# Gated linear attention and a max-out layer on one core: layer 2 per 128-token tile instead of per group of four

## The chip, the cores and the metric

The kernel runs on one core of one Trainium2 chip. The metric is the device time of one execution in microseconds (us); lower is better. Five engines take part: PE (matrix products), DVE (vector), ACT (activations), POOL (elementwise work beside DVE) and SP, which here issues every DMA. Each engine works through its own instructions strictly in program order and waits on semaphores for the others.

## The reference

q, k, v and f_logit are [4 batches, 8 heads, 768 tokens, 48]. A gated linear attention runs over the tokens, then a layer with two weight matrices, a maximum and an output product runs on its result x of [3072 tokens, 384].

```python
f = 1.0 / (1.0 + np.exp(-f_logit))
for t in range(S):
    state = f[:, :, t, :, None] * state + np.einsum('bhd,bhe->bhde', k[:, :, t], v[:, :, t])
    y[:, :, t] = np.einsum('bhd,bhde->bhe', q[:, :, t], state)
...
h1 = x @ w1
h2 = x @ w2
g = np.maximum(h1, h2)
return (g @ w_out).astype(np.float32)
```

w1 and w2 are [384, 1024], w_out is [1024, 384].

## The kernel before, in words

The work is cut into 24 tiles of 128 tokens. Tile i is chunk c = i // 4 of batch b = i % 4, so that four tiles in a row are the same chunk of the four batches, and the state of a batch is needed again four tiles later.

**Attention of a tile**, in six stages. `s_ell(i)` (L198 to L201): ACT makes e = exp(-f) and ell = ln(e + 1), the negative logarithm of the gate, and DVE casts v to vb. `s_cum(i)` (L208 to L221): PE sums ell over the tokens with a triangular matrix (cum, and four short matmuls for the total), ACT takes ei, ed and fl from it, and POOL scales k and q to kp and qp. `s_tr(i)` (L230, L234): PE transposes kp and qp in eight 128x128 pieces, and DVE copies them out as trs. `s_a(i)` (L245, L248): eight matmuls a, which DVE multiplies with the mask into am. `s_y(i)` (L260 to L280): the new state (sa on PE, tmp on DVE, st on POOL), then y from the old state and am, which ACT casts to x. `s_xT(i)` (L290, L291): three transposes of x, copied out by DVE as xT.

**Layer 2** uses max(h1, h2) = relu(h1 - h2) + h2. With wd = w1 - w2 and the product w2o = w2 @ w_out, the output is relu(x @ wd) @ w_out + x @ w2o. So the weights first go through preparation: w2 and w_out are cast, w2 is transposed (w2T, 24 transposes and 8 copies), w2o is multiplied (24 matmuls), wd is subtracted. After that a group of four tiles (512 tokens) takes 24 matmuls d of 512 columns (L156), eight relu casts gT on ACT (L158), and per tile 11 matmuls o of 384 columns (L172), a copy ob and an output DMA.

**Order.** The program order is the order in which the code calls the stages; nothing reorders it. A loop from i = -4 to 23 calls s_y(i), s_tr(i+2), s_a(i+1), s_cum(i+3), s_xT(i), s_ell(i+4) and load(i+8), and between them `unit()` takes the next piece of layer 2 from a queue: first the preparation pieces, then, after each fourth tile, the eight d and eight half o pieces of that group. The preparation pieces come before the first s_ell. What is left in the queue runs after the loop.

**Buffers.** The loaded q, k, v and f tiles have five buffers. In PSUM, a ring of three buffers (`ps_s`) serves cum, tr, sa, y and xtp, one (`ps_a`) serves a, and three (`ps_m`) serve layer 2. The input DMAs of tiles 0 to 2, then w2, w_out, tile 3, w1 and tile 4 are issued first.

Of the kernel before, what the change touches and what calls it, by code (L numbers as in the profile page):

```python
# [4 lines left out]

# [12 lines left out]
def kernel(  # L18
# [62 lines left out]
    ut = consts.tile([C, C], BF16)  # L81
    make_upper_triangular(nc, ut, 1.0, diag=True)
    ident = consts.tile([C, C], BF16)
    make_identity(nc, ident)
    ones_col = consts.tile([C, 1], BF16)
    nc.gpsimd.memset(ones_col, 1.0)
    NQ = 3
# [15 lines left out]
    w2_h = consts.tile([C, JG, d_ff], BF16, name="w2_h")
# [30 lines left out]
    for j in range(JG):
        units.append(lambda j=j: u_w2_cast(j))
    for h in range(4):
        units.append(lambda h=h: u_wo_cast(h))
    for f in range(FG):
        units.append(lambda f=f: u_w2T(f))
    for j in range(JG):  # L140
        units.append(lambda j=j: u_w2o(j))
    for j in range(JG):
        units.append(lambda j=j: u_wd(j))
    N_PREP = len(units)


    xT_g = {}

    def push_group(g):
        gT = work.tile([C, FG, GT], BF16, name="gT", tag="gT")  # L150
        xT = xT_g[g]

        def u_d(f):
            ps = ps_m.tile([C, GT], F32, name="d", tag="mm")
# [5 lines left out]
        hold = {}  # L160

        def u_o(b, half):
            ts = slice(b * C, (b + 1) * C)
            if half == 0:
                hold[b] = ps_m.tile([C, dm], F32, name="o", tag="mm")
            ps = hold[b]
            mms = [(xT[:, j, ts], w2o[:, j, :]) for j in range(JG)]
            mms += [(gT[:, f, ts], wo[:, f, :]) for f in range(FG)]
            cut = 6
            todo = range(0, cut) if half == 0 else range(cut, len(mms))  # L170
            for n in todo:
                nc.tensor.matmul(out=ps, lhsT=mms[n][0], rhs=mms[n][1],  # L172
                                 start=(n == 0), stop=(n == len(mms) - 1))
            if half == 1:
                ob = work.tile([C, dm], F32, name="ob", tag="ob", bufs=3)
                nc.vector.tensor_copy(ob, ps)  # L176
                r0 = b * S + g * C
                nc.sync.dma_start(out=out[r0:r0 + C, :], in_=ob)

        for f in range(FG):  # L180
            units.append(lambda f=f: u_d(f))
        for b in range(B):
            units.append(lambda b=b: u_o(b, 0))
            units.append(lambda b=b: u_o(b, 1))

    def unit(n=1):
        for _ in range(n):
            if units:
                units.popleft()()


    st = {}

    def s_ell(i):
        t = ld[i]
        e = work.tile([C, dm], F32, name="e", tag="e")
# [4 lines left out]
        nc.vector.tensor_copy(vb, t["v"].rearrange("p h d -> p (h d)"))  # L201
        st[i] = {"ell": ell, "v": vb}

    def s_cum(i):
# [76 lines left out]
        s["x"] = x  # L281

    def s_xT(i):
        c, b = divmod(i, B)
        s = st.pop(i)
        if b == 0:
            xT_g[c] = work.tile([C, JG, GT], BF16, name="xT", tag="xT", bufs=3)
# [3 lines left out]
        nc.vector.tensor_copy(xT_g[c][:, :, b * C:(b + 1) * C], ps)  # L291


    for i in range(-4, T):
        if i >= 0:
            s_y(i)
        unit()
        if 0 <= i + 2 < T:
            s_tr(i + 2)
        unit()  # L300
        if 0 <= i + 1 < T:
            s_a(i + 1)
        unit()
        if 0 <= i + 3 < T:
            s_cum(i + 3)
        unit()
        if i >= 0:
            s_xT(i)
        if i < B:
            unit()  # L310
            unit()
        if i >= 0 and i % B == B - 1:
            push_group(i // B)
        if 0 <= i + 4 < T:
# [35 lines left out]
```

## Time and profile before

| | us |
|---|---|
| median of 3 runs | 185.81 |
| lowest and highest of them | 185.0 and 186.49 |
| the profiled execution | 185.38 |
| its span, first to last instruction | 183.6 |
| PE busy in it | 138.6 |
| DVE, ACT, POOL busy | 102.5, 86.1, 75.7 |

An execution's time is a little longer than the span of its instructions. Busy times overlap between engines, so they don't add up to the span. Matmuls are pipelined: the row of one matmul shows its whole passage, and the spacing of starts shows the rate.

### The profile page before, as it was taken

How to read it: one execution, taken by the hardware profiler on the slowest of the kernel's cores; microseconds unless marked ns; L12 is line 12 of the kernel's file. 1: busy time of each engine (PE TensorE's matmuls, PEld its weight loads, DVE VectorE, ACT ScalarE, POOL GpSimd, SP SyncE). 2: the span in 40 equal slices, each digit the busy share in tenths (PEclk: the TensorE clock that was granted, in tenths of full speed). 3: DMA queues.
4: the chain of work that ended last, by engine and by line, in shares of the span. 5: the costliest groups of instructions: out<-in, count | busy, mean ns of one | idle time of the engine just before them, and what ended most of it. 6: DMA issues, size and time to landing. Idle time of an engine off the chain costs nothing.

```text
span 183.6 us, 3633 instructions
## 1 busy us (share of the span) xinstructions
PE 138.6 (75%) x1373; PEld 85.4 (46%) x1384; DVE 102.5 (56%) x161; ACT 86.1 (47%) x200; POOL 75.7 (41%) x107
## 2 busy tenths in 40 slices
PE   0000208946778989999999998999899988998992
PEld 0000106534555545655456654665556654564560
DVE  8200605389777576686676676766776744452031
ACT  2000074483555675446744577346873376412700
POOL 8200004646666366544466544566544644000000
PEclk9999999985555999999999999999999999999999
DMA  6999999999999997698996999969801120022022
GB/s 114 194 185 347 373 199 362 186 187 171 194 189 190 164 191 131 165 209 174 195 151 164 215 172 186 172 142 216 152 0 43 50 86 0 4 87 86 0 89 86
DMA packets 105154, 28.56 MB, mean 156 GB/s; under 512 B 100272, under 2 KB 104368, under 8 KB 105136
## 3 DMA queue, kind: packets, MB, share of 16 engines
q1 hardware_dynamic: 105136, 28.32, 77.1%
q8 instruction: 11, 0.18, 0.5%
q14 instruction: 7, 0.06, 0.1%
HBM read 23.59 MB, written 4.72 MB: 154 GB/s over the span
## 4 chain that ended last, share of the span: by engine, by line
issue 39%; PE 32%; POOL 23%; ACT 3%; POOLq 1%; DVE 1%; ACTq 0%
PE o L172 13%; POOL qp L221 11%; POOL kp L220 9%; PE d L156 9%; PE tr L230 6%; PE a L245 2%; POOL st L98 1%; ACT ei L216 1%; PE y L272 1%; ACT ed L217 1%; PE y L277 1%; ACT gT L158 1%; POOLq L345 1%; POOL ell L94 0%; PE cum L208 0%
## 5 line engine op out<-in xcount | busy, mean ns | idle before, releaser
L220 POOL TENSOR_TENSOR kp<-kt,ei 128x384 bf16<-128x384 f32 x24 | 24.9, 1036 | 76.4 <-issue 38.9
L156 PE MATMUL d<-xT,wd 128*128 128x512 bf16 x133 | 36.7, 383 | 2.3 <-DVE xT L291 1.1
L158 ACT ACTIVATE gT<-d 128x512 bf16<-128x512 f32 x48 | 29.0, 605 | 19.0 <-PE d L156 18.5
L172 PE MATMUL o<-wo,gT 128*128 128x384 bf16 x192 | 37.7, 326 | 0.0
L234 DVE COPY trs<-tr 128x1024 bf16<-128x1024 bf16 x24 | 16.6, 692 | 25.8 <-PE tr L230 25.7
L248 DVE TENSOR_TENSOR am<-a,mask 128x1024 bf16<-128x1024 f32 x24 | 29.3, 1219 | 2.9 <-PE a L245 2.9
L216 ACT ACTIVATE ei<-cum 128x384 f32<-128x384 f32 x24 | 11.7, 489 | 38.2 <-PE cum L210 38.2
L221 POOL TENSOR_TENSOR qp<-qt,ed 128x384 bf16<-128x384 f32 x24 | 27.6, 1148 | 0.0
L176 DVE COPY ob<-o 128x384 f32<-128x384 f32 x24 | 13.4, 558 | 23.3 <-PE o L172 22.4
L172 PEld LDWEIGHTS <-gT 128*128 128x128 bf16 x192 | 17.8, 98 | 10.4
L267 POOL TENSOR_TENSOR st<-tmp,fl 64x192 bf16<-64x192 f32 x40 | 20.0, 501 | 2.3 <-DVE tmp L264 0.8
L124 PE MATMUL w2tp<-ident,w_h 128*128 128x128 bf16 x24 | 3.5, 308 | 21.0 <-DVE w_h L112 21.0
L201 DVE CAST vb<-vt 128x384 bf16<-128x384 f32 x24 | 16.9, 703 | 0.0
L156 PEld LDWEIGHTS <-wd 128*128 128x128 bf16 x144 | 11.8, 98 | 10.8 <-issue 2.3
L172 PE MATMUL o<-w2o,xT 128*128 128x384 bf16 x72 | 15.7, 327 | 0.0
L230 PE MATMUL tr<-ident,qp 128*128 128x128 bf16 x96 | 10.6, 239 | 5.8 <-POOL qp L221 5.0
L277 PE MATMUL y<-vb,am 128*128 128x48 bf16 x192 | 12.0, 190 | 2.2 <-DVE am L248 1.4
L116 ACT CAST wo<-wo_f 128x768 bf16<-128x768 f32 x4 | 3.1, 824 | 21.9 <-DMA wo_f<-in_moe_w_out_dram 21.9
L208 PE MATMUL cum<-ell,ut 128*128 128x384 bf16 x24 | 8.9, 369 | 6.0 <-ACT ell L199 6.0
L277 PEld LDWEIGHTS <-am 128*128 128x128 bf16 x192 | 10.3, 101 | 6.4 <-DVE xT L291 3.7
L280 ACT CAST x<-y 128x384 bf16<-128x384 f32 x24 | 11.2, 467 | 4.2 <-PE y L277 4.1
L199 ACT ACTIVATE ell<-e 128x384 bf16<-128x384 f32 x24 | 12.5, 523 | 0.9
(42 smaller groups left out, 185.1 us busy)
## 6 DMA issues: line engine op xcount, KB each, us to landing
ft<-in_f_logit_dram SPq DMA_DIRECT2D x24, 192.0 KB, 4.3
kt<-in_k_dram SPq DMA_DIRECT2D x24, 192.0 KB, 4.2
qt<-in_q_dram SPq DMA_DIRECT2D x24, 192.0 KB, 4.2
vt<-in_v_dram SPq DMA_DIRECT2D x24, 192.0 KB, 4.3
out_dram<-ob SPq DMA_DIRECT2D x24, 192.0 KB, 2.0
w_f<-in_moe_w_dram SPq DMA_DIRECT2D x2, 1536.0 KB, 7.7
wo_f<-in_moe_w_out_dram SPq DMA_DIRECT2D x1, 1536.0 KB, 11.0
```

Source lines behind the costliest of these rows:

```text
L156: nc.tensor.matmul(out=ps, lhsT=wd[:, j, f * C:(f + 1) * C], rhs=xT[:, j, :], start=(j == 0), stop=(j == JG - 1))
L158: nc.scalar.activation(gT[:, f, :], ps, AF.Relu)
L172: nc.tensor.matmul(out=ps, lhsT=mms[n][0], rhs=mms[n][1], start=(n == 0), stop=(n == len(mms) - 1))
L201: nc.vector.tensor_copy(vb, t["v"].rearrange("p h d -> p (h d)"))
L216: nc.scalar.activation(ei, ps[:, 0:dm], AF.Exp)
L220: nc.gpsimd.tensor_mul(kp[:, :, 0:D], t["k"], ei.rearrange("p (h d) -> p h d", h=H))
L221: nc.gpsimd.tensor_mul(qp[:, :, 0:D], t["q"], ed.rearrange("p (h d) -> p h d", h=H))
L230: nc.tensor.transpose(out=ps[:, n, p, :], in_=src[:, 2 * p:2 * p + 2, :].rearrange("p h d -> p (h d)"), identity=ident)
L234: nc.vector.tensor_copy(tr, ps)
L248: nc.vector.tensor_mul(am.rearrange("p o n c -> p (o n) c"), ps.rearrange("p o n c -> p (o n) c"), mask)
L267: nc.gpsimd.tensor_mul(new[r, :, e], tmp[r, :, e], s["fl"][r, :].unsqueeze(2).to_broadcast([DP, NP, D]))
L277: nc.tensor.matmul(out=y[:, ds], lhsT=am[:, o, p, :], rhs=vb[:, ds], start=(c == 0), stop=(c == 0 or o == 1))
```

## The change

Layer 2 is no longer done for a group of four tiles. Each tile gets its own d (24 matmuls of 128 columns in two halves, into PSUM tiles of 4 x 128 columns, with one relu cast for each half) and its own o, one step behind its attention (LAG = 1). The queue of pieces is gone; the order is written out. Before the loop stand tile 0 and tile 1 with all of their attention, then the whole preparation of the weights, then the early stages of tiles 2 to 5 with layer 2 of tile 0 between them. In the loop s_cum(i+3) comes first.

The input DMAs now bring tiles 0 and 1, then the weights in eight pieces, then tiles 2 to 5; the load buffers are nine instead of five, and a step issues load(i+6) instead of load(i+8). kp and qp have four buffers instead of three. The clearing of ell, st and ones_col moves from POOL to DVE, and qp of tile 0 is made on DVE.

```diff
-    loads = ctx.enter_context(tc.tile_pool(name="loads", bufs=5))
+    loads = ctx.enter_context(tc.tile_pool(name="loads", bufs=9))
...
-    for i in range(3):
-        load(i)
-    nc.sync.dma_start(out=w2_f, in_=moe_w2.rearrange("(j p) ff -> p j ff", p=C))
-    nc.sync.dma_start(out=wo_f, in_=moe_w_out.rearrange("(j p) dm -> p j dm", p=C))
+    load(0)
+    load(1)
+    for j in range(JG):
+        load_w(w2_f, moe_w2, j)
+    for j in range(0, FG, 4):
+        load_w(wo_f, moe_w_out, j, 4)
+    for j in range(JG):
+        load_w(w1_f, moe_w1, j)
+    load(2)
     load(3)
-    nc.sync.dma_start(out=w1_f, in_=moe_w1.rearrange("(j p) ff -> p j ff", p=C))
     load(4)
+    load(5)
...
+    NQ = 4
...
+    for t in ell_b:
         nc.vector.memset(t, 0.0)
-    for t in ell_b:
-        nc.gpsimd.memset(t, 0.0)
...
+    nc.vector.memset(ones_col, 1.0)
+    make_upper_triangular(nc, ut, 1.0, diag=True)
+    make_identity(nc, ident)
+    for t in kp_b + qp_b:
+        nc.vector.memset(t, 0.0)
+    nc.vector.tensor_copy(mask, ut.unsqueeze(1).to_broadcast([C, H, C]))
     for b in range(B):
         for t in st_b[b]:
-            nc.gpsimd.memset(t, 0.0)
...
+            nc.vector.memset(t, 0.0)
...
+    def u_d(i, half):
+        s = st[i]
+        if half == 0:
+            s["g"] = work.tile([C, FG, C], BF16, name="gT", tag="gT")
+        ps = ps_m.tile([C, 4, C], F32, name="d", tag="mm")
+        for n in range(4):
+            f = half * 4 + n
             for j in range(JG):
-                nc.tensor.matmul(out=ps, lhsT=wd[:, j, f * C:(f + 1) * C], rhs=xT[:, j, :],
+                nc.tensor.matmul(out=ps[:, n, :], lhsT=wd[:, j, f * C:(f + 1) * C], rhs=s["xT"][:, j, :],
                                  start=(j == 0), stop=(j == JG - 1))
-            nc.scalar.activation(gT[:, f, :], ps, AF.Relu)
...
+        nc.scalar.activation(s["g"][:, half * 4:half * 4 + 4, :], ps, AF.Relu)
...
-        nc.gpsimd.tensor_mul(qp[:, :, 0:D], t["q"], ed.rearrange("p (h d) -> p h d", h=H))
+        eng = nc.vector if i < 1 else nc.gpsimd
+        eng.tensor_mul(qp[:, :, 0:D], t["q"], ed.rearrange("p (h d) -> p h d", h=H))
...
+    LAG, NPRO = 1, 2
+    s_ell(0)
+    s_v(0)
+    s_cum(0)
+    s_tr(0)
+    s_a(0)
+    s_y(0)
+    s_xT(0)
+    s_ell(1)
+    s_v(1)
+    s_cum(1)
+    s_tr(1)
+    for j in range(JG):
+        u_w2_cast(j)
+    s_a(1)
+    s_y(1)
+    s_xT(1)
+    for f in range(FG):
+        u_w2T(f)
+    for h in range(4):
+        u_wo_cast(h)
+    for j in range(JG):
+        u_w2o(j)
+    for j in range(JG):
+        u_wd(j)
+    s_ell(2)
+    s_v(2)
+    s_cum(2)
+    s_ell(3)
+    s_v(3)
+    s_tr(2)
+    u_d(0, 0)
+    s_cum(3)
+    s_ell(4)
+    s_v(4)
+    s_a(2)
+    u_d(0, 1)
+    s_tr(3)
+    u_o(0, 0)
+    s_cum(4)
+    s_ell(5)
+    s_v(5)
+    u_o(0, 1)
+    load(6)
+    load(7)
...
+    for i in range(NPRO, T + LAG):
+        m = i - LAG
+        if i + 3 < T:
+            s_cum(i + 3)
+        if i < T:
             s_y(i)
...
+        u_d(m, 0)
+        if i + 2 < T:
             s_tr(i + 2)
...
+        u_d(m, 1)
+        if i < T:
+            s_xT(i)
+        if i + 1 < T:
             s_a(i + 1)
...
+        u_o(m, 0)
+        u_o(m, 1)
+        if i + 4 < T:
             s_ell(i + 4)
-        if 5 <= i + 8 < T:
-            load(i + 8)
...
+            s_v(i + 4)
+        if 6 <= i + 6 < T:
+            load(i + 6)
```

The first place is PE in the middle of the program, around the matmuls cum of a tile. Before:

```order
L172 MATMUL o<-wo,gT 128x384
L208 LDWEIGHTS ut
L208 MATMUL cum<-ell_141,ut 128x384
L210 LDWEIGHTS ell_141
L210 MATMUL cum<-ones_col,ell_141 128x1
...
L172 LDWEIGHTS gT
L172 MATMUL o<-wo,gT 128x384
```

And in the changed kernel, at the same matmuls:

```order
L162 MATMUL o<-wo,gT 128x384
L191 LDWEIGHTS ut
L191 MATMUL cum<-ell_144,ut 128x384
L193 LDWEIGHTS ell_144
L193 MATMUL cum<-ones_col,ell_144 128x1
...
L244 LDWEIGHTS kp_139
L244 MATMUL sa<-vb,kp_139 128x96
```

Before, cum stands in the middle of a tile's o, behind the transposes and a of its step; now it stands between the last o of a step and sa, the first matmul of the next s_y, ahead of all transposes of its step.

The second place is ACT at the start of the program. Before:

```order
L54 ACT_TABLE_LOAD
L116 CAST wo<-wo_f 128x768 x3
L198 ACTIVATE e<-ft 128x384
L199 ACTIVATE ell_140<-e 128x8x48
L116 CAST wo<-wo_f 128x768
L216 ACTIVATE ei<-cum 128x384
```

And in the changed kernel, from the cast of x of tile 0 on:

```order
L264 CAST x<-y 128x384
L177 ACTIVATE e<-ft 128x384
L178 ACTIVATE ell_144<-e 128x8x48
L199 ACTIVATE ei<-cum 128x384
L200 ACTIVATE ed<-cum 128x384
L201 ACTIVATE fl<-cum 128x4
L264 CAST x<-y 128x384
L121 CAST wo<-wo_f 128x768 x4
L137 CAST w2o<-w2op 128x384 x3
L177 ACTIVATE e<-ft 128x384
```

The casts of w_out (wo) stood ahead of the first tile's e; now they stand behind x of tile 1, and e of tile 1 stands behind x of tile 0.

The third place is SP's queue in the changed kernel, around the first output DMA:

```order
L63 DMA ft_127<-in_f_logit_dram 128x8x48
L63 DMA kt_129<-in_k_dram 128x8x48
L63 DMA qt_131<-in_q_dram 128x8x48
L63 DMA vt_133<-in_v_dram 128x8x48
L169 DMA out_0_dram<-ob_540 128x384
L63 DMA ft_543<-in_f_logit_dram 128x8x48
L63 DMA kt_545<-in_k_dram 128x8x48
```

The output of tile 0, which waits for ob of tile 0, stands ahead of the loads of tiles 6 and 7; the rows above it are the loads of tile 5.

## Rows read from the trace of the kernel before

**Rows 1.** Windows: us, busy us (instructions) of each engine, granted clock, DMA share, GB/s
```profile
2.00:4.00 2.00, 0.00 (x0) 0.00 (x0) 2.00 (x3) 0.01 (x1) 2.00 (x6) 1.00 1.04 201
...
18.00:19.00 1.00, 0.00 (x0) 0.00 (x0) 0.00 (x0) 0.00 (x0) 0.00 (x0) 1.00 0.99 390
...
50.00:55.00 5.00, 3.68 (x40) 2.58 (x40) 3.91 (x7) 2.73 (x8) 3.52 (x6) 0.50 1.38 191
...
80.00:100.00 20.00, 18.69 (x208) 11.69 (x209) 13.06 (x22) 13.19 (x32) 11.63 (x15) 1.00 0.95 177
```
The five engines in these rows are PE, PE's weight loads, DVE, ACT and POOL.

**Rows 2.** Order of time, the start: start us, length us, what, idle before and releaser
```profile
0.74 0.43 SPq L65 DMA_DIRECT2D ft<-in_f_logit_dram  x1
...
2.42 3.48 DVE L100 COPY mask<-ut 128x1024 bf16<-128x1024 bf16 x1
...
19.58 1.90 DVE L112 CAST w_h<-w_f 128x1024 bf16<-128x1024 f32 x3 [13.69 <-DMA w_f<-in_moe_w_dram]
...
23.93 2.30 ACT L116 CAST wo<-wo_f 128x768 bf16<-128x768 f32 x3 [21.92 <-DMA wo_f<-in_moe_w_out_dram]
...
32.13 4.57 PE L130 MATMUL w2op<-wo,w2T 128*128 128x384 bf16 x24
```

**Rows 3.** Order of time, one period of the slow stretch
```profile
51.32 0.61 PE L230 MATMUL tr<-ident,qp 128*128 128x128 bf16 x4 [0.47 <-POOL qp L221]
...
52.40 0.50 PE L208 MATMUL cum<-ell,ut 128*128 128x384 bf16 x1
...
53.08 0.49 ACT L216 ACTIVATE ei<-cum 128x384 f32<-128x384 f32 x1 [2.24 <-PE cum L210]
...
53.70 1.01 POOL L220 TENSOR_TENSOR kp<-kt,ei 128x384 bf16<-128x384 f32 x1 [1.40 <-issue]
...
54.66 1.12 POOL L221 TENSOR_TENSOR qp<-qt,ed 128x384 bf16<-128x384 f32 x1
...
55.84 0.61 PE L230 MATMUL tr<-ident,qp 128*128 128x128 bf16 x4 [0.46 <-POOL qp L221]
```

**Rows 4.** Order of time, PE alone, one step of the even middle
```profile
120.16 0.20 PE L272 MATMUL y<-st,trs 128*128 128x96 bf16 x1
...
120.53 0.65 PE L172 MATMUL o<-w2o,xT 128*128 128x384 bf16 x3
...
121.50 0.39 PE L230 MATMUL tr<-ident,kp 128*128 128x128 bf16 x4
121.95 0.40 PE L230 MATMUL tr<-ident,qp 128*128 128x128 bf16 x4
122.18 0.98 PE L172 MATMUL o<-wo,gT 128*128 128x384 bf16 x5
123.09 0.40 PE L245 MATMUL a<-trs 48*128 48x128 bf16 x8
...
125.90 0.20 PE L272 MATMUL y<-st,trs 128*128 128x96 bf16 x1
```

**Rows 5.** Groups by line: busy us, mean ns of one, idle before
```profile
L248 DVE TENSOR_TENSOR am<-a,mask 128x1024 bf16<-128x1024 f32 x24 | 29.3, 1219 | 2.9 <-PE a L245 2.9
L234 DVE COPY trs<-tr 128x1024 bf16<-128x1024 bf16 x24 | 16.6, 692 | 25.8 <-PE tr L230 25.7
...
L199 ACT ACTIVATE ell<-e 128x384 bf16<-128x384 f32 x24 | 12.5, 523 | 0.9
...
L156 PEld LDWEIGHTS <-wd 128*128 128x128 bf16 x144 | 11.8, 98 | 10.8 <-issue 2.3
...
L291 DVE COPY xT<-xtp 128x384 bf16<-128x384 bf16 x24 | 8.4, 352 | 5.8 <-PE xtp L290 5.8
...
L92 DVE MEMSET qp<- 128x256 uint32 x3 | 0.8, 272 | 0.9 <-PEq L334 0.9
```

**Rows 6.** Order of time, the end
```profile
167.56 5.34 PE L156 MATMUL d<-xT,wd 128*128 128x512 bf16 x23 [0.74 <-DVE xT L291]
...
180.08 0.56 DVE L176 COPY ob<-o 128x384 f32<-128x384 f32 x1 [1.23 <-PE o L172]
```

More of the change, by code (lines that the diff above doesn't have):

```diff
@@ L2 @@
 logging.getLogger("concourse").setLevel(logging.ERROR)
-from collections import deque
 from contextlib import ExitStack
@@ L43 @@
     T = nch * B
-    GT = B * C
     ctx.enter_context(tc.manual_schedule())
     consts = ctx.enter_context(tc.tile_pool(name="consts", bufs=1))
-    loads = ctx.enter_context(tc.tile_pool(name="loads", bufs=5))
+    loads = ctx.enter_context(tc.tile_pool(name="loads", bufs=9))
     work = ctx.enter_context(tc.tile_pool(name="work", bufs=2))
@@ L70, with load_w @@
     wo_f = consts.tile([C, FG, dm], F32, name="wo_f")
-    for i in range(3):
-        load(i)
-    nc.sync.dma_start(out=w2_f, in_=moe_w2.rearrange("(j p) ff -> p j ff", p=C))
-    nc.sync.dma_start(out=wo_f, in_=moe_w_out.rearrange("(j p) dm -> p j dm", p=C))
+    def load_w(dst, src, j, n=1):
+        nc.sync.dma_start(out=dst[:, j:j + n, :],
+                          in_=src[j * C:(j + n) * C, :].rearrange("(j p) x -> p j x", p=C))
+    load(0)
[7 more added lines that the diff above has]
+    load(2)
     load(3)
-    nc.sync.dma_start(out=w1_f, in_=moe_w1.rearrange("(j p) ff -> p j ff", p=C))
     load(4)
[L81 to L87, printed above, removed]
+    load(5)
+    NQ = 4
     qp_b = [consts.tile([C, H, DP], BF16, name=f"qp{n}") for n in range(NQ)]
@@ L90 @@
     ell_b = [consts.tile([C, H, DP], BF16, name=f"ell{n}") for n in range(2)]
-    for t in qp_b + kp_b:
-        nc.vector.memset(t, 0.0)
-    for t in ell_b:
-        nc.gpsimd.memset(t, 0.0)
-    st_b = [[consts.tile([C, NP, 2 * D], BF16, name=f"st{b}_{n}") for n in range(2)] for b in range(B)]
+    st_b = [[consts.tile([C, NP, 2 * D], BF16, name=f"st{b}_{n}") for n in range(2)] for b in range(B)]
+    ut = consts.tile([C, C], BF16)
+    ident = consts.tile([C, C], BF16)
+    ones_col = consts.tile([C, 1], BF16)
+    mask = consts.tile([C, H, C], BF16, name="mask")
+    for t in ell_b:
+        nc.vector.memset(t, 0.0)
+    nc.vector.memset(ones_col, 1.0)
[4 more added lines that the diff above has]
+    nc.vector.tensor_copy(mask, ut.unsqueeze(1).to_broadcast([C, H, C]))
     for b in range(B):
         for t in st_b[b]:
-            nc.gpsimd.memset(t, 0.0)
-    mask = consts.tile([C, H, C], BF16, name="mask")
-    nc.vector.tensor_copy(mask, ut.unsqueeze(1).to_broadcast([C, H, C]))
+            nc.vector.memset(t, 0.0)
     w2_h = consts.tile([C, JG, d_ff], BF16, name="w2_h")
@@ L107 @@
     w2o = consts.tile([C, JG, dm], BF16, name="w2o")
-    units = deque()
     def u_w2_cast(j):
@@ L132, in u_w2o @@
         nc.scalar.copy(w2o[:, j, :], ps)
[L134 to L154, printed above, removed]
+    st = {}
@@ L160, in push_group @@
[L160 to L192, printed above, removed]
+        nc.scalar.activation(s["g"][:, half * 4:half * 4 + 4, :], ps, AF.Relu)
+    def u_o(i, half):
+        s = st[i]
+        if half == 0:
+            s["o"] = ps_m.tile([C, dm], F32, name="o", tag="mm")
+        mms = [(s["xT"][:, j, :], w2o[:, j, :]) for j in range(JG)]
+        mms += [(s["g"][:, f, :], wo[:, f, :]) for f in range(FG)]
+        cut = 6
+        for n in (range(0, cut) if half == 0 else range(cut, len(mms))):
+            nc.tensor.matmul(out=s["o"], lhsT=mms[n][0], rhs=mms[n][1],
+                             start=(n == 0), stop=(n == len(mms) - 1))
+        if half == 1:
+            c, b = divmod(i, B)
+            ob = work.tile([C, dm], F32, name="ob", tag="ob", bufs=5)
+            nc.vector.tensor_copy(ob, s["o"])
+            r0 = b * S + c * C
+            nc.sync.dma_start(out=out[r0:r0 + C, :], in_=ob)
+            del st[i]
@@ L199, in s_ell, with s_v @@
         nc.scalar.activation(ell[:, :, 0:D], e.rearrange("p (h d) -> p h d", h=H), AF.Ln, bias=1.0)
+        st[i] = {"ell": ell}
+    def s_v(i):
+        t = ld[i]
         vb = work.tile([C, dm], BF16, name="vb", tag="vb", bufs=6)
         nc.vector.tensor_copy(vb, t["v"].rearrange("p h d -> p (h d)"))
-        st[i] = {"ell": ell, "v": vb}
+        st[i]["v"] = vb
     def s_cum(i):
@@ L283, in s_xT @@
     def s_xT(i):
[L284 to L287, printed above, removed]
+        s = st[i]
         ps = ps_s.tile([C, JG, C], BF16, name="xtp", tag="s")
@@ L290, in s_xT @@
             nc.tensor.transpose(out=ps[:, j, :], in_=s["x"][:, j * C:(j + 1) * C], identity=ident)
-        nc.vector.tensor_copy(xT_g[c][:, :, b * C:(b + 1) * C], ps)
-    for i in range(-4, T):
-        if i >= 0:
+        s["xT"] = work.tile([C, JG, C], BF16, name="xT", tag="xT", bufs=5)
+        nc.vector.tensor_copy(s["xT"], ps)
+    LAG, NPRO = 1, 2
[48 more added lines that the diff above has]
+        if i < T:
             s_y(i)
-        unit()
-        if 0 <= i + 2 < T:
+        u_d(m, 0)
+        if i + 2 < T:
             s_tr(i + 2)
-        unit()
-        if 0 <= i + 1 < T:
+        u_d(m, 1)
+        if i < T:
+            s_xT(i)
+        if i + 1 < T:
             s_a(i + 1)
[L303 to L314, printed above, removed]
+        u_o(m, 0)
+        u_o(m, 1)
+        if i + 4 < T:
             s_ell(i + 4)
-        if 5 <= i + 8 < T:
-            load(i + 8)
-    while units:
-        unit()
+            s_v(i + 4)
+        if 6 <= i + 6 < T:
+            load(i + 6)
 _INS = ['q', 'k', 'v', 'f_logit', 'moe_w1', 'moe_w2', 'moe_w_out']
```

## The prediction

> **What bounds the kernel now.** I read the windows by stage first, then the order of time at the start, in the slow stretch, in the even middle and at the end.
>
> At the start nothing is computed for tile 0 before the weights are there. DMA brings the tiles' loads at 201 GB/s, the weights at 390 GB/s [rows 1]; in the order of time, DVE's first cast of w2 ends a wait of 13.69 us for its DMA, and ACT's casts of wo end one of 21.92 us for theirs, at 23.93 [rows 2]. Tile 0's exponentials stand behind those casts in ACT's order, though f of tile 0 was issued at 0.74.
>
> From 40 to 60 us attention runs alone (layer 2 waits until four tiles are through) with the granted clock at 0.50, the lower level of 1.2 GHz, PE busy 3.68 of 5 us in the row shown, the third of four such [rows 1]. The period is a loop over three engines [rows 3]: PE transposes qp at 51.32, then a, then cum at 52.40, ACT's ei at 53.08, POOL's kp at 53.70 and qp at 54.66, and the next transposes of qp at 55.84: 4.52 us. It closes because cum(i+3) stands on PE behind the transposes of tile i+2, which wait for POOL.
>
> From 60 us on PE is at full clock and busy 18.69 of 20 us [rows 1]. The step at 120.16 lasts to 125.90, 5.74 us [rows 4]. The transposes of kp and qp start 0.45 apart, and four need 121.95 to 122.18, 0.23: so 0.22 is a wait for qp, the same loop. At the end the last group's layer 2 stands alone: d from 167.56, the last ob at 180.08 [rows 6], and 3.5 us from there to the span's end, 183.6.
>
> **The steady step, part by part.** A step of the changed kernel has one tile of attention, one tile of d and one of o. Start from the step of 5.74, which has attention and 22 o matmuls (two tiles) and no d [rows 4]:
> - 11 o go. Six took 120.53 to 121.50, 0.162 each: -1.78.
> - 24 d of 128 columns come, each with a weight load of its own, in place of 6 of 512 columns a tile. The nearest rows are the transposes: also 128x128, also one weight load each, 0.23 for four, 0.0575 each: +1.38.
> - cum goes to the head of the step, so kp and qp of tile i+3 have a whole step before PE wants them: the wait of 0.22 goes. PE's small gap before a (five o from 122.18 need 0.81, a starts 0.91 later) I leave in.
>
> 5.74 - 1.78 + 1.38 - 0.22 = 5.12, say 5.1. What is late next? I walked the other queues through such a step. In 80 to 100 us, some 3.6 steps, ACT is busy 13.19 us, DVE 13.06 and POOL 11.63 [rows 1]: 3.7, 3.6 and 3.2 a step, and none gets an instruction more a tile. By my estimate ell(i+4) ends 0.4 us before cum wants it, and DVE's tmp frees its PSUM buffer 0.7 before the transposes of x want it. The tightest is the same ring of three PSUM buffers elsewhere: the transposes of kp and qp reuse cum's, which ACT frees with fl about 0.1 us earlier. A tile's loads (0.79 MB) take 3.9 us at 201 GB/s, and its output, 0.2 MB, some 0.5 if it runs at the weights' 390: 4.4 under 5.1. All are covered by PE, none by much.
>
> How sure is 0.0575? From below, 128 columns cannot beat their share of an o, 0.162/3 = 0.054 (-0.1 a step). From above, the weight load would set the pace.
> The Trainium skill ("TensorE: Matmul & The Clock Gate", section "Back-to-back issue gap") gives about 81 ns as the sustained spacing of 128-column matmuls that each have a weight load; by that, d would cost 1.94 and the step 5.7. The transposes here run at 57.5 ns with a load each, so I go by the row and keep the slower case as a rival.
>
> **The start.** Everything is in program order now: tile 0, then tile 1, then the weight products, then tiles 2 to 4 with layer 2 of tile 0.
> - f of tile 0 is issued as before; with 201 GB/s flowing from 2 us, two such loads of 0.2 MB are in by 4 us, so e(0) starts near 3.6.
> - One tile through attention at half clock [rows 3, 5]: e and ell 0.52 each; cum to ei 0.68; ei to kp 0.62; kp 1.01 (qp, on DVE for this tile, ends some 0.5 later); transposes 0.61; trs 0.69; a 0.6; am 1.22; y 0.55 by estimate; x and its transposes 0.5 each by estimate; xT 0.35; with about 0.05 to 0.1 for each hand-over, 9.3. Tile 0 is through at 12.9.
> - Tile 1 starts on ACT behind x(0), at 12.0. It also takes 9.3, and DVE's three w2 casts stand ahead of its am: 1.90 [rows 2]. By the two rates the loads of tiles 0 and 1 end near 10, w2 is in near 14, wo 18, w1 22: the casts find their data. Tile 1 is through at 23.2.
> - Weight products: eight w2T copies of the size of xT, 0.35 each [rows 5], 2.8; 24 w2op matmuls 4.57 [rows 2]; a last cast 0.5: 31.1. DVE's wd lies beside them.
> - Tile 2 to the transposes of qp: 1.04 + 0.68 + 0.62 + 1.0 + 1.12, 35.7. Then two rounds of the same loop of 4.52 [rows 3] (tiles 3 and 4 still have cum behind the transposes), and half a d of tile 0 in front of the first cum, 12 x 0.115 at half clock, 1.4: 46.1. The main loop starts there.
>
> Unknown here: the mask copy and the memsets moved to DVE. A memset is 0.27 [rows 5]; two for ell, eight for kp and qp, eight smaller ones for st, some 4.4. The mask copy took 3.48 while POOL cleared st beside it [rows 2]. Its bounds: 0.69, a DVE copy of as many elements [rows 5], and 3.48. I take 1.2, as POOL no longer works beside it: DVE is free near 6.6, before qp(0) is wanted; with 3.48 the chain slips 2.3.
> The Trainium skill ("SBUF — State Buffer", section "Who interferes with whom") says that a DVE copy in a two-port mode and GpSimd hold a shared port pair in turn, each blocking the other; by that the copy would fall to the short end. No row of before shows it alone.
>
> A wait is added on SP's queue: out(0) stands ahead of load(6), and waits for ob(0), near 46.4. Behind it are loads 6 and 7; DMA has nothing to do from about 38 on (22 and four tiles of 3.9). At three microseconds to land, as f of tile 0 above, and one more per load, f6 lands near 50 and v6 near 53, against a need at about 51.5 (e(6)) and 53.3 (vb(6)). It just fits; each microsecond more is paid once or twice, up to 4 us.
>
> **The sum.** The step at 46.1 begins at half clock and gets full clock on the way (the clock of before rises between the row of 0.50 and the full row, when layer 2 has come in [rows 1]): 5.1 + 1.4 = 6.5, to 52.6. 17 full steps (tiles 3 to 19) x 5.1 = 86.7: 139.3. Four attention steps that shed sa, cum, tr and a one after the other, each 0.25 to 0.5 less, and a last one with layer 2 alone: 4.85 + 4.6 + 4.1 + 3.8 + 3.2 = 20.5: 159.8. The end as now, 3.5: a span of 163.3. Around its span the profiled execution had 185.38 - 183.6 = 1.8: **165.1 us, forecast 165**, against 185.38 for that execution and a median of 185.81.
>
> Where the 20 us come from: the lone layer 2 at the end falls from 12.5 (167.56 to 180.08) to 3.2, some 9; the rest is the step of 5.74 that becomes 5.1, and the layer 2 of three tiles that is done before tile 4's step, where before all of it is still to come.
>
> **Rivals.**
> 1. Another queue than PE's sets the step (fl late for the transposes, DVE's order, loads that arrive late): for it speaks the 0.1 us of slack at fl, against it that ACT and DVE have over 1 us a step to spare. At 5.5 a step, 20 x 0.4 = 8: 173. Chance 0.14.
> 2. The start takes longer (the mask at 3.48, loads 6 and 7 late, a clock that stays low one step more): +6: 171. Chance 0.11.
> 3. The weight loads pace d. A weight load of d is 0.098 by itself [rows 5], but y's twelve matmuls, each with a load, start at 120.16 and end by 120.53, 0.031 apart [rows 4], which speaks against it. Half way between 0.0575 and 0.098, 24 x 0.02 x 22 steps = 11: 176. With the Trainium skill's 81 ns it would be 12 more, 177. Chance 0.05.
> 4. Slower than before: the clock. At 1.2 GHz a step of 5.1 becomes about 8.8, 3.7 more. Attention alone was held there at 3.68 us busy of 5 [rows 1]. If gaps in the main loop bring it back, six such steps cost 22 us, and from there on the kernel is slower than before: 187 and up. Against it: PE has almost no gap in the step above. Chance 0.04.
> 5. The start goes at full clock from the weight products on: -4: 161. Chance 0.06.
>
> The forecast itself, 161 to 169, has 0.60. The range of 159 to 174 leaves out case 4, most of case 3 and the far side of cases 1 and 2. A measurement of this kernel can tell about 1% from no change. Faster by over 1%: all but case 4 and a little of cases 1 and 3, 0.93; within 1%: 0.03; slower: 0.04.
>
> **What would show it.** Right: tile 0's e near 3.6 us; first d near 36; the first step with d, o and y at 46; steps of 5.1 with PE rows back to back and 12 d in 0.7; POOL's kp and qp done long before their transposes; last d some 7 us before the end. Wrong: 12 d in 0.9 or more (case 3); the clock at 0.5 after 55 us (case 4); a regular wait of PE for fl, trs or a load in the middle (case 1); ei(6) or vb(6) waiting for a DMA (case 2).

## The result, and the profile after

The changed kernel takes 158.33 us, the median of 4 runs (158.02 to 159.27), against 186.15 for the kernel before, run beside it (4 runs, 185.0 to 187.3): a ratio of 0.851 (0.845 to 0.858). The forecast was 165, the range 159 to 174: the direction was right, and the time lies just under the range. The profiled execution of after took 159.27 us with a span of 157.5. The profiled executions of after and of numbers 5, 6 and 10 below are the slowest of theirs, by up to 1.7% over the fastest.

First the head of its page: busy us, share of the span and instructions of each engine, then two rows of the span in 40 slices.

```profile
PE 133.0 (84%) x1816; PEld 103.2 (66%) x1816; DVE 98.0 (62%) x175; ACT 86.8 (55%) x200; POOL 66.9 (43%) x95
...
PE   0253559647699999999999999999999999999991
...
PEclk9999999977999999999999999999999999999998
```

PE is busy 5.6 us less than before (138.6) and idle 24.5 us instead of 45.0. So of the 26.1 us by which the span fell, some 20 are waits of PE that are gone. From the twelfth slice on, at 43 us, PE's slices are full up to the last. The windows (columns as in [rows 1]) say the same by stage:

```profile
2.00:4.00 2.00, 0.00 (x0) 0.00 (x0) 1.99 (x8) 0.38 (x2) 0.00 (x0) 1.00 1.05 204
30.00:35.00 5.00, 1.39 (x13) 0.97 (x13) 0.36 (x1) 3.27 (x8) 1.95 (x2) 0.87 1.25 197
35.00:40.00 5.00, 3.91 (x49) 3.22 (x47) 2.28 (x3) 2.84 (x7) 1.96 (x2) 0.79 1.11 156
40.00:45.00 5.00, 3.77 (x51) 2.69 (x49) 2.07 (x4) 3.10 (x10) 2.61 (x3) 1.00 0.26 66
...
80.00:100.00 20.00, 20.00 (x305) 16.06 (x302) 14.07 (x23) 13.39 (x34) 11.70 (x17) 1.00 0.95 197
```

In the middle PE is busy 20.00 of 20 us at full clock, against 18.69 in the same stretch of [rows 1]; DVE and ACT keep 6 us of slack. The long stretch at 0.50 between 40 and 60 us is gone: in the windows from 30 us on the clock dips between 30 and 40 only. Ahead of the weight products the slices of PEclk say 9 too, but the rows say half speed: cum takes 0.48 us at 4.77 below, and 0.33 in the loop. Why the two differ there is not shown; for the start I go by the rows.

The start, in order of time (columns as in [rows 2]):

```profile
3.52 0.36 DVE L104 COPY mask<-ut 128x1024 bf16<-128x1024 bf16 x1
3.64 0.52 ACT L177 ACTIVATE e<-ft 128x384 f32<-128x384 f32 x1 [1.62 <-DMA ft<-in_f_logit_dram]
...
4.77 0.48 PE L191 MATMUL cum<-ell,ut 128*128 128x384 bf16 x1 [4.77 <-ACT ell L178]
...
13.01 0.36 DVE L273 COPY xT<-xtp 128x384 bf16<-128x384 bf16 x1 [1.21 <-PE xtp L271]
...
22.61 0.36 DVE L273 COPY xT<-xtp 128x384 bf16<-128x384 bf16 x1 [1.21 <-PE xtp L271]
...
30.36 0.53 ACT L177 ACTIVATE e<-ft 128x384 f32<-128x384 f32 x1
...
31.49 0.32 PE L191 MATMUL cum<-ell,ut 128*128 128x384 bf16 x1 [1.54 <-ACT ell L178]
...
34.62 0.61 PE L214 MATMUL tr<-ident,qp 128*128 128x128 bf16 x4 [0.35 <-POOL qp L205]
35.02 1.49 PE L150 MATMUL d<-xT,wd 128*128 128x128 bf16 x12
...
36.30 0.53 PE L191 MATMUL cum<-ell,ut 128*128 128x384 bf16 x1
...
37.28 0.84 PE L150 MATMUL d<-xT,wd 128*128 128x128 bf16 x12
...
39.61 0.40 PE L214 MATMUL tr<-ident,qp 128*128 128x128 bf16 x4 [0.56 <-POOL qp L205]
...
40.82 0.33 PE L191 MATMUL cum<-ell,ut 128*128 128x384 bf16 x1
...
43.27 0.32 PE L191 MATMUL cum<-ell,ut 128*128 128x384 bf16 x1 [1.21 <-ACT ell L178]
```

Tile 0's e starts at 3.64, its xT at 13.01, tile 1's at 22.61. The cum at 31.49, 36.30, 40.82 and 43.27 are those of tiles 2 to 5; the last opens the main loop. The row of one matmul tells the level of the clock: cum takes 0.53 us at 36.30 and 0.33 at 40.82, and twelve d take 1.49 at 35.02 and 0.84 at 37.28. So PE got its full clock near 37 us.

PE in the second step of the loop, from one cum to the next (columns as in [rows 4]):

```profile
48.26 0.33 PE L191 MATMUL cum<-ell,ut 128*128 128x384 bf16 x1
48.43 0.24 PE L193 MATMUL cum<-ones_col,ell 128*128 128x1 bf16 x4
48.53 0.33 PE L244 MATMUL sa<-vb,kp 128*128 128x96 bf16 x4
48.70 0.36 PE L261 MATMUL y<-vb,am 128*128 128x48 bf16 x8
48.90 0.83 PE L150 MATMUL d<-xT,wd 128*128 128x128 bf16 x12
49.76 0.38 PE L214 MATMUL tr<-ident,kp 128*128 128x128 bf16 x4
49.98 0.39 PE L214 MATMUL tr<-ident,qp 128*128 128x128 bf16 x4
50.20 0.83 PE L150 MATMUL d<-xT,wd 128*128 128x128 bf16 x12
50.87 0.33 PE L271 MATMUL xtp<-ident,x 128*128 128x128 bf16 x3
51.13 0.40 PE L229 MATMUL a<-trs 48*128 48x128 bf16 x8
51.46 0.66 PE L162 MATMUL o<-w2o,xT 128*128 128x384 bf16 x3
51.96 1.46 PE L162 MATMUL o<-wo,gT 128*128 128x384 bf16 x8
53.26 0.33 PE L191 MATMUL cum<-ell,ut 128*128 128x384 bf16 x1
```

A step is 5.00 us (48.26 to 53.26), and no row has a wait behind it. The transposes of kp and qp start 0.22 apart, where [rows 4] have 0.45. Twelve d take 50.20 to 50.87, 0.67 us, 0.0558 each. The first step, 43.27 to 48.26, took 4.99. The eighteen from 43.27 to the last cum, at 133.74, make 90.5, 5.03 each: sixteen take 5.0, one 5.25 and one 5.29. The end:

```profile
150.87 1.50 PE L150 MATMUL d<-xT,wd 128*128 128x128 bf16 x24
...
152.70 1.46 PE L162 MATMUL o<-wo,gT 128*128 128x384 bf16 x8
154.20 0.56 DVE L167 COPY ob<-o 128x384 f32<-128x384 f32 x1 [2.57 <-PE o L162]
```

Layer 2 now stands alone from 150.87 to the last ob at 154.20, 3.3 us instead of the 12.5 of [rows 6].

### The profile page after: what moved, and what is told of

Its sections match the earlier page's. It is cut to its first block, busy times and chain, and to the rows that moved or that the text cites. A ratio compares the mean times of both kernels' runs of the same rounds, so it can differ in the third digit from the quotient of the medians.

```text
span 157.5 us, 4506 instructions
## 1 busy us (share of the span) xinstructions
PE 133.0 (84%) x1816; PEld 103.2 (66%) x1816; DVE 98.0 (62%) x175; ACT 86.8 (55%) x200; POOL 66.9 (43%) x95
## 4 chain that ended last, share of the span: by engine, by line
PE 69%; issue 7%; DMA 6%; POOL 5%; DVE 4%; ACT 4%; SPq 2%; POOLq 0%; ACTq 0%
PE o L162 25%; PE d L150 17%; PE tr L214 6%; DMA vt<-in_v_dram 6%; PE a L229 4%; PE w2op L135 3%; PE y L261 3%; PE xtp L271 3%; POOL qp L205 2%; SPq L63 2%; PE cum L191 2%; PE sa L244 2%; PE y L256 2%; POOL kp L203 2%; PE w2tp L129 2%
## 5 line engine op out<-in xcount | busy, mean ns | idle before, releaser
L203 POOL TENSOR_TENSOR kp<-kt,ei 128x384 bf16<-128x384 f32 x24 | 24.0, 999 | 57.7 <-issue 31.7
L150 PE MATMUL d<-xT,wd 128*128 128x128 bf16 x576 | 40.1, 221 | 0.0
L162 PE MATMUL o<-wo,gT 128*128 128x384 bf16 x192 | 35.3, 326 | 0.0
L150 PEld LDWEIGHTS <-wd 128*128 128x128 bf16 x576 | 33.9, 99 | 0.2
L162 PEld LDWEIGHTS <-gT 128*128 128x128 bf16 x192 | 18.7, 98 | 12.3
L167 DVE COPY ob<-o 128x384 f32<-128x384 f32 x24 | 13.4, 558 | 18.2 <-PE o L162 18.2
L205 POOL TENSOR_TENSOR qp<-qt,ed 128x384 bf16<-128x384 f32 x23 | 23.4, 1018 | 0.0
L264 ACT CAST x<-y 128x384 bf16<-128x384 f32 x24 | 11.9, 496 | 18.8 <-PE y L261 18.8
L184 DVE CAST vb<-vt 128x384 bf16<-128x384 f32 x24 | 10.6, 443 | 7.9 <-DMA vt<-in_v_dram 7.8
L214 PE MATMUL tr<-ident,kp 128*128 128x128 bf16 x96 | 9.9, 229 | 5.9 <-POOL kp L203 5.7
L177 ACT ACTIVATE e<-ft 128x384 f32<-128x384 f32 x24 | 12.5, 519 | 1.6 <-DMA ft<-in_f_logit_dram 1.6
L273 DVE COPY xT<-xtp 128x384 bf16<-128x384 bf16 x24 | 8.5, 355 | 7.4 <-PE xtp L271 5.1
L178 ACT ACTIVATE ell<-e 128x384 bf16<-128x384 f32 x24 | 12.5, 523 | 0.8
L193 PEld LDWEIGHTS <-ell 128*128 128x128 bf16 x96 | 6.1, 99 | 10.2 <-issue 7.7
```

What stands on the lines that cost most here:

```text
L150: nc.tensor.matmul(out=ps[:, n, :], lhsT=wd[:, j, f * C:(f + 1) * C], rhs=s["xT"][:, j, :], start=(j == 0), stop=(j == JG - 1))
L162: nc.tensor.matmul(out=s["o"], lhsT=mms[n][0], rhs=mms[n][1], start=(n == 0), stop=(n == len(mms) - 1))
L167: nc.vector.tensor_copy(ob, s["o"])
L205: eng.tensor_mul(qp[:, :, 0:D], t["q"], ed.rearrange("p (h d) -> p h d", h=H))
L214: nc.tensor.transpose(out=ps[:, n, p, :], in_=src[:, 2 * p:2 * p + 2, :].rearrange("p h d -> p (h d)"), identity=ident)
```

## The experiments

All eleven are the changed kernel with one edit, or with those of an earlier one and one more. Ratios are to the kernel before, so 0.851 stands for no difference from after.

**1. cum back behind the transposes.**

```diff
-        if i + 3 < T:
-            s_cum(i + 3)
...
         u_o(m, 0)
+        if i + 3 < T:
+            s_cum(i + 3)
         u_o(m, 1)
```

> The changed kernel, with cum(i+3) of a loop step moved from the head of the step to between the two halves of o, so again behind the transposes and a; nothing else changes. Theory (a loop): cum, ei, kp, qp, the transposes, then d, a and half an o in front of the next cum close a loop over PE, ACT and POOL: 0.5 + 0.6 + 2.0 + 2.7 = 5.8 us a step in place of 5.0, some 16 us more, 174 us, with PE waiting for qp in front of its transposes in each step. Rival (the term of the prediction): the place of cum is worth only the wait of 0.22 us a step that the trace of before showed, 4 to 5 us, 163.

172.86 us (one run), span 171.1. PE alone in the middle:

```profile
99.92 0.21 PE L256 MATMUL y<-st,trs 128*128 128x96 bf16 x1
...
100.96 0.39 PE L214 MATMUL tr<-ident,kp 128*128 128x128 bf16 x4
101.93 0.40 PE L214 MATMUL tr<-ident,qp 128*128 128x128 bf16 x4 [0.58 <-POOL qp L205]
...
104.41 0.33 PE L191 MATMUL cum<-ell,ut 128*128 128x384 bf16 x1
...
105.66 0.21 PE L256 MATMUL y<-st,trs 128*128 128x96 bf16 x1
```

The step is 5.74 again (99.92 to 105.66). The transposes start 0.97 apart instead of 0.22, and those 0.75 are the difference from 5.00. The loop of [rows 3] sets the step: from the transposes of qp at 101.93 PE needs 2.48 to come to cum, and ACT and POOL then take the rest. This is the largest single part of the change, some 14 us. The kernel before has these rows behind the transposes of qp at 121.95 [rows 4]:

```profile
124.41 0.33 PE L208 MATMUL cum<-ell,ut 128*128 128x384 bf16 x1
...
125.65 0.33 PE L260 MATMUL sa<-vb,kp 128*128 128x96 bf16 x4
```

There PE needs 2.46 from the transposes to cum, so the step has the same length, though PE has less to do in it now. In this order the matmuls that are saved elsewhere in the step are worth nothing; only those between the transposes and cum count.

**2. The weights' preparation ahead of tiles 0 and 1**, with the input DMAs as in after.

```diff
     LAG, NPRO = 1, 2
+    for j in range(JG):
+        u_w2_cast(j)
+    for f in range(FG):
+        u_w2T(f)
...
     s_ell(0)
...
-    for f in range(FG):
-        u_w2T(f)
```

> The changed kernel, with the whole preparation of the weights called ahead of the attention of tiles 0 and 1; DMA order and loop unchanged. Theory (the start is a chain of work): attention of two tiles, 3.6 to 23 us in the changed kernel, then stands behind the products on ACT and DVE: e of tile 2 moves from 30.4 to some 43, the run takes 13 us more, 171. Rival (the start is set by the arrival of loads and weights, so the order of its work is free): within 2 us of 158.

171.58 us (one run), span 169.8; the loop starts at 55.13 instead of 43.27, and the windows from 30 to 50 show a clock of 0.50. The span grew by 12.3, of it 11.9 before the loop. Tiles 0 and 1 fill the time in which the weights are loaded.

**3. Layer 2 of tile 0 behind the early stages of tiles 2 to 5**, and **4. a lag of four steps**, with layer 2 of tile 0 in the loop like the others (and a sixth buffer for xT).

```diff
     s_tr(2)
-    u_d(0, 0)
...
     s_v(5)
+    u_d(0, 0)
+    u_d(0, 1)
+    u_o(0, 0)
     u_o(0, 1)
```

```diff
-    LAG, NPRO = 1, 2
+    LAG, NPRO = 4, 2
...
-        u_d(m, 0)
+        if m >= 0:
+            u_d(m, 0)
```

> The changed kernel, with d and o of tile 0 moved from between the early stages of tiles 2 to 4 to behind them, just ahead of the loop; same work. Theory (layer 2 between the tiles holds the clock up): without it attention runs alone from 31 to 41 us and the granted clock stays at 0.5 there and into the first step, as it did in the kernel before; the first step with y starts at 46 or later in place of 43.3, and the run takes 3 to 5 us more, 161 to 163. Rival (the clock is up because of the weight products, and d and o only fill time in which PE waits): clock unchanged, 3 us more at most for the 3.2 us of d and o that no longer hide behind POOL.

> The changed kernel with LAG = 4 in place of 1: layer 2 of a tile comes four steps behind its attention, none of it in the start (xT gets a buffer more). Theory (the end is only the other side of the start: PE's work is the same, and what counts is where PE has nothing else to do): four tiles of layer 2 stand alone at the end, 12.6 us in place of 3.2, and the first three steps and the start lose their filling; attention alone also runs at the lower clock, so that they become hardly shorter: 7 to 9 us more, 165 to 167. Rival (the lag is free as long as PE is full in the middle): within 2 us of 158.

161.18 us, ratio 0.865 (0.860 to 0.871), and 164.66 (one run). The windows of the first, then of the second:

```profile
35.00:40.00 5.00, 3.93 (x40) 3.23 (x41) 2.40 (x3) 3.15 (x10) 3.04 (x4) 0.50 1.12 168
40.00:45.00 5.00, 4.97 (x57) 3.66 (x56) 1.64 (x3) 2.77 (x8) 1.74 (x2) 0.81 0.08 23
```

```profile
40.00:45.00 5.00, 3.96 (x45) 2.92 (x44) 3.44 (x5) 3.06 (x8) 4.00 (x6) 0.50 1.44 188
45.00:50.00 5.00, 4.25 (x54) 3.49 (x55) 3.13 (x6) 3.35 (x10) 4.25 (x6) 0.50 1.02 170
```

Layer 2 among the first stages is worth about 3 us. In number 3 the loop starts no later than in after (43.05); my expectation of 46 or later missed. But the next cum waits 1.14 for ell, and from tile 2's transposes of qp to that cum it takes 15.82 (33.54 to 49.36) instead of 13.64 (34.62 to 48.26). How much of this is the lower clock and how much the lost filling, the run doesn't separate. With a lag of four PE runs attention alone up to 50 us with gaps and at 0.50, as in [rows 1], and three more tiles of layer 2 stand at the end: some 6 us.

**5. Five load buffers instead of nine.**

```diff
-    loads = ctx.enter_context(tc.tile_pool(name="loads", bufs=9))
+    loads = ctx.enter_context(tc.tile_pool(name="loads", bufs=5))
```

> The changed kernel with five load buffers in place of nine. Theory (a step issues load(i+6) at its end, and the tile five before it, i+1, has been read by then): no wait is added, within 1% of 158. Rival (the four more buffers feed the loop): loads start later, DVE waits for v in the steps, 3 us or more.

159.51 us, 0.854 (0.848 to 0.860): no difference, as expected. Its trace holds more than that, and is taken up under number 11.

**6. The input DMAs in the order of before**, the weights in whole pieces.

```diff
     load(0)
     load(1)
+    load(2)
+    load_w(w2_f, moe_w2, 0, JG)
+    load_w(wo_f, moe_w_out, 0, FG)
+    load(3)
+    load_w(w1_f, moe_w1, 0, JG)
...
-    load(2)
-    load(3)
     load(4)
```

> The changed kernel with the input DMAs in the order and the pieces of before: tiles 0 to 2, w2 whole, w_out whole, tile 3, w1 whole, tiles 4 and 5. Theory (compute sets the start; w2 is then in at 18, w_out at 22, w1 at 30): the w2 casts at 17.9 wait under 1 us, the wo casts hardly, wd ends at 33 instead of 29, still ahead of d at 35: within 1.5 us of 158. Rival (the pieces and their place make the start): 4 us or more.

162.8 us, 0.873 (0.867 to 0.879): my expectation fell, and the rival held. In order of time:

```profile
20.46 1.90 DVE L114 CAST w_h<-w_f 128x1024 bf16<-128x1024 f32 x3 [2.61 <-DMA w_f<-in_moe_w_dram]
22.28 1.22 DVE L229 TENSOR_TENSOR am<-a,mask 128x1024 bf16<-128x1024 f32 x1
...
33.81 4.30 DVE L121 TENSOR_TENSOR wd<-w_f 128x1024 bf16<-128x1024 f32 x3 [5.73 <-DMA w_f<-in_moe_w_dram]
...
36.99 1.97 POOL L202 TENSOR_TENSOR qp<-qt,ed 128x384 bf16<-128x384 f32 x1
...
39.02 0.61 PE L211 MATMUL tr<-ident,qp 128*128 128x128 bf16 x4 [1.32 <-POOL qp L202]
39.42 0.85 PE L147 MATMUL d<-xT,wd 128*128 128x128 bf16 x6
```

Two waits of DVE make it. Its w2 casts hold up tile 1's am, which stands behind them, and all that follows up to cum of tile 2, which starts at 34.24 instead of 31.49. Then wd, after its wait of 5.73 us for w1, runs beside kp and qp of tile 2 on POOL, which take 1.67 and 1.97 us, against 1.00 each in after, where wd is done before them; a piece of wd takes 1.43 instead of 1.16. That the two slow each other is read from these rows; no run tried it alone. So the transposes of qp start at 39.02 instead of 34.62, and the first d right behind them, at 39.42 instead of 35.02. DMA's order is worth about 4.5 us because DVE is in program order too.

**7 to 10. Can the start be shorter?** Number 7 (the first edit below) puts gate and cum of tile 2 and the gate of tile 3 between the weight products; 8 also issues loads 6 and 7 right behind load 5, ahead of the first output (the second edit); 9 is this second edit alone; 10 is 8 with the stages of tiles 0 and 1 interleaved.

```diff
-    for j in range(JG):
-        u_w2o(j)
+    s_ell(2)
+    u_w2o(0)
+    s_cum(2)
+    u_w2o(1)
+    s_ell(3)
+    u_w2o(2)
     for j in range(JG):
         u_wd(j)
-    s_ell(2)
     s_v(2)
-    s_cum(2)
-    s_ell(3)
+    s_tr(2)
     s_v(3)
-    s_tr(2)
```

```diff
     load(5)
+    load(6)
+    load(7)
...
     u_o(0, 1)
-    load(6)
-    load(7)
```

> An attempt to beat both: e, ell and cum of tile 2 and e, ell of tile 3 stand between the three weight products w2o instead of behind all of them, so that POOL makes kp and qp of tile 2 while PE multiplies the weights. Theory (the start is a chain through ACT, PE and POOL up to the loop): the transposes of tile 2 move from 34.6 to about 30.5 and the loop starts 4 us earlier, 154. Rival (loads: v6 lands at about 49 already and the loads would now be late for the loop): less than 1 us gained, with waits of DVE or PE for loads in the first steps.

> The kernel of e7 with load(6) and load(7) issued right behind load(5) at the start of the program instead of behind the output of tile 0 (nine buffers hold them). Theory (e7's loop started at 38.6 instead of 43.3, but its second step then waited for f6, because loads 6 and 7 stood on SP's queue behind out(0), which waits for ob(0): DMA ran at 124 GB/s from 40 to 45 and the step took 7.5 us): f6 now lands near 39, the second step takes 5, and the 4 us of e7 come through: 154. Rival (DMA's rate itself is short there, the queue's order doesn't matter): within 1 us of e7's 158.

> The changed kernel with load(6) and load(7) issued right behind load(5), nothing else. Theory (in the changed kernel PE is full from the loop's first step at 43.3 on, so the waits of DVE for v of tile 6 hurt nobody): within 1% of 158. Rival (the late loads cost something already): 1.5 us or more gained.

> The kernel of e8 with the attention of tiles 0 and 1 interleaved at the start (e, ell and cum of tile 1 ahead of a and y of tile 0) instead of one after the other. Theory (the start is a chain of hand-overs, and engines are idle beside it): tile 1 is through at 17 to 18 instead of 23, the weight products end at 25 instead of 29, but from there the loads set the pace (f of tile 5 lands at 35.7): the loop starts 1.5 to 2 us before that of e8, 152. Rival (the loads set the start already): as e8 within 0.5 us.

| | us | ratio | loop starts | second cum |
|---|---|---|---|---|
| after | 158.33 | 0.851 (0.845 to 0.858) | 43.27 | 48.26 |
| 7 | 157.99 | 0.849 (0.843 to 0.855) | 38.63 | 46.12 |
| 8 | 155.27 | 0.833 (0.828 to 0.837) | 38.64 | 44.18 |
| 9 | 159.24 | 0.853 (0.848 to 0.859) | 43.16 | 48.16 |
| 10 | 155.28 | 0.832 (0.828 to 0.836) | 38.61 | 46.22 |

Number 7 starts the loop 4.6 us earlier and gives 2.5 of it back in its first step, which takes 7.49 instead of 4.99. The median gains 0.3, which can't be told from nothing:

```profile
44.99 0.52 ACT L177 ACTIVATE e<-ft 128x384 f32<-128x384 f32 x1 [2.96 <-DMA ft<-in_f_logit_dram]
46.12 0.32 PE L191 MATMUL cum<-ell,ut 128*128 128x384 bf16 x1 [2.33 <-ACT ell L178]
```

f of tile 6 is late, since its load stands behind the output of tile 0 on SP. Number 8 removes that and is, level with number 10, the best version of this study, 3 us under after; 9 shows that the same edit is worth nothing while there is no early start to feed. In 10 the expected further gain didn't come: the loop starts no earlier, cum(5) waits 2.89 for ell, and its e 1.65 for its load. There the loads set the start. And behind that wait of PE the granted clock of its trace is 0.50, from 38 to 44 us:

```profile
40.00:45.00 5.00, 5.00 (x46) 4.20 (x45) 3.19 (x6) 2.71 (x7) 2.91 (x4) 0.52 0.94 148
```

So its first step, most of it at half clock, takes 7.61 us without a wait of PE, against 5.54 in number 8. The medians of the two kernels are level all the same.

**11. PE kept busy between cum(2) and the transposes**, where PE of after waits 1.77 us for kp, by 30 matmuls whose result nobody reads.

```diff
     s_cum(2)
+    warm = ps_m.tile([C, 4, C], F32, name="warm", tag="mm")
+    for n in range(30):
+        nc.tensor.matmul(out=warm[:, n % 4, :], lhsT=w2_h[:, 0, 0:C], rhs=w2_h[:, 0, 0:C],
+                         start=True, stop=True)
```

> The changed kernel with 30 matmuls more (128 columns, w2 with itself, the result is not used) behind cum of tile 2, where PE waits for POOL at 31.9 to 33.7; this only keeps PE at work. It tests the step of the prediction on the clock. Theory (PE's half clock in the start and in the first step costs little, since the chain there is hand-overs on ACT, POOL and DVE): granted clock 1.0 throughout 30 to 45, the loop starts at 42 to 42.5 instead of 43.3, at most 1.2 us gained, 157.5. Rival (the prediction's price: half clock against full is worth 1.4 in the first step and some 1.6 in the two rounds before it): 3 us, 155.5.

158.89 us, 0.852 (0.847 to 0.857): not to be told from after, though the granted clock is 1.00 in every window from 30 us on. Numbers 5 and 9 have the PE order of after and a clock that stayed low longer. So four executions can be compared over one stretch: from the transposes of qp of tile 2 to those of tile 3, and on to the loop's first cum.

| | clock 30:35, 35:40, 40:45 | tr(2) to tr(3) | tr(3) to the loop |
|---|---|---|---|
| 5 | 0.75, 0.50, 0.73 | 34.00 to 39.00: 5.00 | to 43.98: 4.98 |
| 9 | 0.80, 0.51, 1.00 | 34.21 to 39.20: 4.99 | to 43.16: 3.96 |
| after | 0.87, 0.79, 1.00 | 34.62 to 39.61: 4.99 | to 43.27: 3.66 |
| 11 | 1.00, 1.00, 1.00 | 34.56 to 38.74: 4.18 | to 42.41: 3.67 |

```profile
35.00:40.00 5.00, 4.66 (x44) 3.64 (x42) 2.29 (x4) 2.90 (x7) 1.96 (x2) 0.50 1.21 160
```

```profile
35.00:40.00 5.00, 3.63 (x52) 2.71 (x50) 2.87 (x4) 2.84 (x7) 1.97 (x2) 1.00 0.99 162
```

The first row is of number 5, the second of 11: at full clock PE does more matmuls in less busy time and then waits, since ACT and POOL set the pace. From half to full clock the whole stretch falls from 9.98 to 7.85, 2.1 us; after, with its rise near 37, has 1.3 of these, all in the second part. Number 2, whose clock is at 0.50 up to 50 us and 0.61 from there to 55, has the same two times as number 5 in the same order of work: 5.00 (45.15 to 50.15) and 4.98 (to 55.13).

## Why the prediction was right, and where it failed

The reading of before held: the start waiting for weights, the loop of three engines, and the lone layer 2 at the end are each gone in the trace of after, and experiments 1, 2 and 4 bring them back one at a time, at some 14, 13 and 6 us. (The edits overlap, so these don't add up.) By the steps of the sum:

- **The price of d** held: 0.0558 us against 0.0575 from the transposes. Rival 3, the weight loads as pace, fell, and the 81 ns of the Trainium skill ("TensorE: Matmul & The Clock Gate", section "Back-to-back issue gap") don't agree with this trace, where 128-column matmuls with a load each keep 56 ns.
- **The step**, 5.12 by the sum and set at 5.1, was 5.03 on average: -1.2 over the 17 steps (48.26 to 133.74 against 86.7). Most steps took 5.0. Of the sum's error some 0.08 lies between the first sa and the first y, 0.25 us in before (125.65 to 125.90) and 0.17 here (48.53 to 48.70), a gap that the sum had left in; up to 0.04 is d. No other queue set it (rival 1).
- **"The wait of 0.22 goes"** was right in the sum and wrong in weight. I put moving cum beside the removal of 11 o as a small term of its own. Experiment 1 shows that without it the step stays at 5.74: the move is what lets the other terms count. It is worth 0.75 a step.
- **Tiles 0 and 1** came out close: xT of tile 0 ends at 13.4 against 12.9, of tile 1 at 23.0 against 23.2. The mask copy took 0.36, under my lower bound of 0.69, and was hidden. Rival 2 had two more causes: loads 6 and 7 late, and a lasting low clock. Experiment 9 excludes the first for this order, and the second wasn't there in after.
- **The failed step is "the step at 46.1 begins at half clock and gets full clock on the way", and the half clock in "the start" that leads up to it.** I had tile 2's transposes of qp at 35.7, the loop at 46.1 and its second step at 52.6. The trace has 34.62, 43.27 and 48.26, 4.3 us earlier in all. Of these, 1.1 lie before the transposes: ACT's e(2) starts at 30.36 and not 31.1, and the chain behind it takes 4.3 and not 4.6. The stretch to the loop took 8.65 instead of 10.4, -1.75. Experiments 5, 9 and 11 split that: at half clock it would have been 9.98, so 1.3 is the clock, which rose near 37 us; only 0.4 is the counting of "two rounds of the same loop" and half a d. The last 1.5 are the first step at full clock, 4.99 for 6.5. So some 2.8 of the 4.3 come from the place where I put the clock's rise. The price that I gave a first step at half clock, 1.4, was too low besides: number 10 has a step most of which runs at half clock, at 7.61. In after the clock was up before the loop began, so that this price was never paid.
- **The two rounds** were nearly the right size for a wrong reason. In the first, a no longer stands inside the loop as in [rows 3] but behind cum, and d takes its room: 5.00 even at half clock, not 4.52 + 1.4. The second is no round: cum(5) opens the main loop ahead of the transposes of tile 4 and waits for ell(5) alone, 2.45 behind cum(4); but o of tile 0 stands before cum(4), and at half clock the two make up 4.98.
- **Rival 5**, full clock from the weight products on, at 161 with a chance of 0.06, came nearest: behind the weight products PE ran at half clock only from tile 2's transposes to about 37 us.
- **The last five steps** took 20.4 (133.74 to the end of the last o, near 154.2) against 20.5, and the end 3.3 against 3.5. Rival 4 didn't occur: the windows from 40 us on have a clock of 1.00.

Together: -2.8 for the loop's start, -1.5 for the first step, -1.2 for the 17 steps, -0.1 and -0.2 at the end: 5.8, from a span of 163.3 to 157.5. All have one sign. The range was drawn from mishaps, which all cost time; below it held rival 5's 161 and two microseconds more, which the smaller terms together used up. The profiled execution, 159.27, still lies inside the range, and the median, 158.33, just outside: that difference is scatter between executions, the 5.8 us of the sum are not.

## What to carry to other kernels

When a loop over several engines closes through one engine's program order, first move the instruction that closes it; until then, removing work from that engine gains nothing unless the work lies inside the loop. Where the granted clock rises at the start is an unknown to be priced on both sides, below the sum too. A shorter start pays only if the loads can feed it: look at what stands ahead of them on the issuing queue.

## What the runs showed that I had not expected

- The mask copy of 128x1024 took 3.48 us beside POOL's memsets [rows 2] and 0.36 with POOL idle: a factor of ten. This agrees with the Trainium skill ("SBUF — State Buffer", section "Who interferes with whom"), which has such a DVE copy and GpSimd block each other, though the change moved more than this one neighbour and no run took it away alone.
- The clock's rise comes at different places in the same order of PE instructions: near 37 us in after, in number 9 between the transposes at 39.20, which take 0.61 us, and cum at 40.71 (0.33), and in number 5 between 41.32, where cum takes 0.53 us, and 43.98, where it takes 0.32. In all three PE had worked from tile 2's transposes of qp up to the rise with no gap over 0.4 us. Why the rise comes where it does was not tried.
- Full clock through the whole start brought the loop forward by 0.9 us (42.41 against 43.27) and gave nothing that the times can tell: where ACT and POOL set the pace, a faster PE only waits longer.
